# Attention and a mixture of experts on one core: tokens stored as two 16-bit planes and turned by transfers

## The chip, the core and the metric

The kernel runs on one core of a Trainium2 chip, as one launch. The metric is the device time in microseconds, the median of timed runs. The engines are TensorE (PE in the rows; its weight loads are PEld), VectorE (DVE), ScalarE (ACT), GpSimd (POOL) and SyncE (SP), which here only issues transfers.

## The reference

A local-global attention (4 batches, 8 heads, 768 positions, 64 per head) gives x of 3072 tokens by 512. A gate picks two of eight experts for each token, and the experts' outputs are added with the gate's weights:

```python
logits = x @ w_gate
noisy = logits + np.log1p(np.exp(x @ w_noise)) * noise
top2 = np.argpartition(-noisy, 2, axis=1)[:, :2]
...                                   # softmax over the two: top2_w
for e in range(8):
    for k in range(2):
        mask = top2[:, k] == e
        h = np.maximum(x[mask] @ w1[e], 0.0)          # 512 -> 1024
        out[mask] += top2_w[mask, k, None] * (h @ w2[e])
```

## The kernel before, in words

Attention runs over 24 blocks of 128 tokens, in steps of two pairs of heads; a written order (the loop over `n`, with `at`, `tick` and `finish`) puts routing steps between its matmuls. `gate_t(g)` stores block g of x to the DRAM tensor `xd` (rows of 512 float32) from SP and turns it on TensorE for the gate; `gate_l` and `gate_s` finish the gate's logits. `route(r)` turns the logits of a segment of blocks into lists of token rows per expert. Segment 2 (`CLOSE`, up to block 16) closes the first 512 tokens of expert 0, and four gathers fetch them by GpSimd's indirect transfers (`gather`, `xg`).

Each expert works on a fixed number of tokens (812 down to 768), in tiles of 128: 7 tiles for experts 0 to 4, 6 for the last three. Expert 0 is done plainly: `turn` transposes a gathered tile on TensorE, four 128x128 blocks into one PSUM bank, and ScalarE and VectorE split it into a high and a low part (`xh`, `xl`); `up(c, f)` and `down(0, t)` are its two products. Each product is three passes of matmuls on the split parts.

Experts 1 to 7 use a product of seven block products in place of eight (`first`, with `TERMS`), which wants sums of blocks of the tokens and of the weights. `tokens(e, t)` takes tiles t and t + 3 (for t = 3 tile 6 alone), transposes them on TensorE (the loops at L1229 and L1235) and makes the sums t1 to t4 on VectorE, with the parts cut by ScalarE and VectorE (`cut`, L194 and L195). `weights(e, c)` does the like with GpSimd's subtractions (L1189 to L1192). `first(e, before)` loops over four blocks c of features; in each, `between(c, slot)` runs the jobs of a table `ahead` at slots 4 to 7, between products of six matmuls. `second(e)` runs the down products, and between them spreads `prepare(e + 1)`, the list of jobs that makes the next expert's tokens. `put` scales a result and adds it to the output rows by GpSimd's indirect transfers.

Every engine takes its instructions in the order in which the program is written; waits are by semaphores between engines. SP's queue holds the loads of weights (`load_w`, four `raw` buffers), the stores of x and the clearing of the output. GpSimd's queue holds gathers, scatters, the weights' sums and, for segments 0 to 2, the routing masks (L505). The stores of a block wait for the last of its heads (`norm`, L837); the next user of the same `ys` buffer waits for the store. The last part, a loop under `tc.If(left > 0)`, serves tokens beyond an expert's capacity; it did not run.

Of the kernel before, what the change touches and what calls it, by code (L numbers as in the profile page):

```python
# [15 lines left out]
U32 = mybir.dt.uint32  # L16
AF = mybir.ActivationFunctionType
# [3 lines left out]
P = 128  # L21
# [13 lines left out]
def tile_local_global_attention_then_moe(  # L35
# [51 lines left out]
    xd = dram.tile([N + DUMP, Dm], F32, name="xd")  # L87
# [120 lines left out]
    xg = {}  # L208
# [10 lines left out]

    def gather(e, t, n=DUMP + N):  # L220
        if e >= E or t >= tiles(e):
            return
        r = rows(e, t)[0]
        xg[e, t] = gp.tile([r.shape[0], Dm], F32, name="xg", bufs=5)
        nc.gpsimd.indirect_dma_start(  # L225
            out=xg[e, t], out_offset=None, in_=xd[:n],
            in_offset=bass.IndirectOffsetOnAxis(ap=r, axis=0),
            bounds_check=n - 1, oob_is_err=False)

# [6 lines left out]
    def rank():  # L236
# [4 lines left out]
        more_ = gp.tile([P, Dm], F32, name="xg", bufs=5)[:, :n * n].rearrange("p (r e) -> p r e", r=n)  # L241
# [11 lines left out]
        for x in range(2):  # L253
            b = gp.tile([P, Dm], F32, name="xg", bufs=5)[:, :n * n * TT].rearrange("p (r t e) -> p r t e", r=n, t=TT)
# [6 lines left out]
    def rest():  # L261

        x = gp.tile([P, Dm], F32, name="xg", bufs=5)
# [18 lines left out]
    def turn(e, t, ps=None):  # L282
        if t >= tiles(e):
            return
        x = xg.pop((e, t))
# [16 lines left out]
    XR, XT, LS = {}, {}, {}  # L302
# [30 lines left out]
    def gate_l(g):  # L333
        j = partner(g)
# [56 lines left out]
    def route(r):  # L391
# [135 lines left out]
        def marks(i):  # L527
            b = gp.tile([P, Dm], F32, name="xg", bufs=5)
# [36 lines left out]
        if r == CLOSE:  # L565
# [14 lines left out]
    with ExitStack() as actx:  # L580
# [126 lines left out]
        def empty_rows():  # L707
            nc.gpsimd.memset(zero, 0.0)
            o = xd[:DUMP].rearrange("(p r) d -> p r d", p=P)
            nc.sync.dma_start(o, zero[:, None, :].to_broadcast(o.shape))  # L710
# [297 lines left out]
    with ExitStack() as mctx:  # L1008
# [51 lines left out]
        def put(e, t, ps):  # L1060
# [4 lines left out]
            ins = nc.gpsimd.indirect_dma_start(  # L1065
                out=out, out_offset=bass.IndirectOffsetOnAxis(ap=r, axis=0),
                in_=y, in_offset=None, bounds_check=N + DUMP - 1, oob_is_err=True, compute_op=OP.add)
            for o in added[e]:
                tc.declare_no_dep(ins.ins, o.ins, reason="an expert's tokens are all different")
            added[e].append(ins)  # L1070
# [4 lines left out]
        def down(e, t):  # L1075
# [6 lines left out]
            for f in features if e else range(FC):  # L1082
# [3 lines left out]
                if n == 3 * FC:  # L1086
                    put(e, t, ps)
# [123 lines left out]
        def tokens(e, t, banks):  # L1211
# [11 lines left out]
            def one():  # L1223
                if t < 3:
                    x1, x2 = (bank_at(banks.pop(0)).rearrange("p (k t) -> p k t", k=KC) for _ in range(2))
                    for ps, j in ((x1, t), (x2, t + 3)):
                        x = xg.pop((e, j))
                        for k in range(KC):
                            nc.tensor.transpose(ps[:, k], x[:, k * P:(k + 1) * P], ident)  # L1229
                else:  # L1230
                    x = xg.pop((e, 6))
                    r = x.shape[0]
                    ps = bank_at(banks.pop(0))[:, :KC * r].rearrange("p (k t) -> p k t", k=KC)
                    for k in range(KC):
                        nc.tensor.transpose(ps[:, k], x[:, k * P:(k + 1) * P], ident[:r, :r])  # L1235
                    x1, x2 = ps[:, :, :r // 2], ps[:, :, r // 2:]
# [4 lines left out]
                if t < 2:  # L1241
                    gather(e, fetch[5 + t])
# [4 lines left out]
            def two():  # L1247
# [3 lines left out]
                nc.vector.tensor_sub(t3, t2, t3)  # L1251
# [6 lines left out]

        def prepare(e):
            if e == 1:  # L1260
                banks = [3, 1, 0, 4, 1]
                return pair[1:] + [y for t in (1, 2, 3) for y in tokens(1, t, banks)]
            banks = [1, 2, 3, 7, 0, 4, 1]
            w = [x for c in range(2) for x in weights(e, c)]
            x = [tokens(e, t, banks) for t in range(3 + (tiles(e) > 6))]
            x = [[lambda a=a, b=b: (a(), b()), c, d] for a, b, c, d in x]
            todo = [w[0], *x[0], w[1], *x[1], *x[2]]
            if tiles(e) > 6:
                todo += x[3]
            return todo + [w[2]]  # L1270

        for t in range(3):
            for i, _ in enumerate(down(0, t)):
                if (t, i) == (2, 1):
                    for j in range(TB):
                        turn(0, TA + j, bank("sc") if j == TB - 1 else None)
                    for j in fetch[:5]:
                        gather(1, j)
        w0, w1_ = weights(1, 0), weights(1, 1)
        pair = tokens(1, 0, [2, 7])  # L1280
        ready = {0: w0[0], 1: w1_[0], 3: w0[1], 4: w1_[1], 5: w0[2], 6: w1_[2]}
        for f in range(FC):
            if f == FC - 1:
                pair[0]()
            up(1, f)
            if f in ready:
                ready[f]()
# [36 lines left out]
        def first(e, before):  # L1324
# [21 lines left out]
            def get(j):  # L1346
                return lambda: gather(e + 1, fetch[j])

            ahead = {
                (0, 4): [w[1][0]], (0, 5): [w[1][1], get(0)], (0, 6): [w[1][2], w2_(0)], (0, 7): [w2_(4)],  # L1350
# [175 lines left out]
```

## Time and profile before

| | |
|---|---|
| timed runs | 730.53, 729.93, 729.34 us; median 729.93 |
| the profiled execution, first to last instruction | 730.6 us, 16343 instructions |
| TensorE busy / its weight loads | 708.1 us (97%) / 636.3 us (87%) |
| VectorE, ScalarE, GpSimd busy | 452.6, 397.7, 275.7 us |
| granted TensorE clock | 0.994 mean |
| sizes of transfers | first load of k 464 KB, of q 256 KB; a block of x 256 KB |

The times of stages are read from the busy times of windows: attention until 140 us, the first expert's up and down products until some 220, then a pattern of a preparation (some 23 us) and four blocks of features (some 48 us) per expert, and a tail from 675 us. In rows of the chain the first number is the start, the second the time on the chain; in rows of instructions the first is the start, the second the duration, and the bracket at the end the idle time before it with what ended it. In rows of groups a mean in ns stands before the second bar.

### The profile page before, as it was taken

What the parts mean: (1) busy time and instruction counts of PE and PEld (TensorE: products, weight loads), DVE (VectorE), ACT (ScalarE), POOL (GpSimd) and SP (SyncE); (2) the same over time, 40 slices, a digit from 0 to 9 for tenths busy, and PEclk for the clock granted to TensorE, in tenths of its full rate; (3) what the DMA queues carried; (4) which work ended last, traced back from release to release, by engine and by line L of the source; (5) the groups of instructions that cost most, each with busy time, mean ns of one, the idle gap of its engine ahead of it and who ended that gap; (6) DMA issues with size and microseconds to landing.
All of it is one profiled execution on the core that took longest, in us unless ns stands there. A gap on an engine that the chain in (4) does not pass through costs nothing.

```text
span 730.6 us, 16343 instructions
## 1 busy us (share of the span) xinstructions
PE 708.1 (97%) x5953; PEld 636.3 (87%) x5953; DVE 452.6 (62%) x1473; ACT 397.7 (54%) x901; POOL 275.7 (38%) x292
## 2 busy tenths in 40 slices
PE   7999999999999999999999999999999999999993
PEld 5878888777899999999989998999898899889983
DVE  7668788858947487457636762766367557637500
ACT  6888787652335564456445644655455446445510
POOL 2230404410182463255436524551645345442221
PEclk9999999999999999999999999999999999999997
DMA  9996779962082463246443634471446436533243
GB/s 268 315 307 194 231 221 310 285 227 106 23 242 78 55 177 96 55 96 146 117 67 103 147 95 75 130 172 32 88 144 148 85 86 146 128 59 88 29 49 42
DMA packets 84393, 99.75 MB, mean 137 GB/s; under 512 B 6100, under 2 KB 51284, under 8 KB 84304
## 3 DMA queue, kind: packets, MB, share of 16 engines
q1 hardware_dynamic: 72896, 72.53, 32.0%
q0 software_dynamic: 11264, 25.83, 19.8%
q8 instruction: 49, 0.80, 0.5%
q10 hardware_dynamic: 144, 0.26, 0.2%
q14 instruction: 40, 0.33, 0.1%
HBM read 71.01 MB, written 27.59 MB: 135 GB/s over the span
## 4 chain that ended last, share of the span: by engine, by line
PE 65%; issue 6%; POOL 3%; DVE 3%; ACT 2%; DMA 1%; POOLq 0%; ACTq 0%; DVEq 0%
PE av L1084 23%; PE bank L1337 22%; PE av L1107 9%; PE bank L1229 3%; PE at L1054 2%; PE sc L1054 2%; POOL out_dram L1065 2%; PE av L821 1%; DVE wall L195 1%; PE bank L1130 1%; DMA out_dram<-zero,ids 1%; DVE w2l L195 1%; ACT hh L1035 1%; POOL wall L505 1%; PE at L800 1%
## 5 line engine op out<-in xcount | busy, mean ns | idle before, releaser
L1337 PE MATMUL bank<-xh,wall 128*128 128x384 f32 (+4 forms) x784 | 215.6, 342 | 0.8 <-DVE aside L1370 0.6
L1337 PEld LDWEIGHTS bank<-xh,wall 128*128 128x128 f32 x784 | 143.4, 188 | 5.6 <-DVE wall L195 1.4
L1337 PE MATMUL bank<-xl,wall 128*128 128x384 f32 (+4 forms) x392 | 133.4, 340 | 0.0
L1065 POOL DMA_INDIRECT out_dram<-y,ids x40 | 62.8, 1570 | 154.2 <-ACT y L1064 123.1
L1084 PE MATMUL av<-w2h,hh 128*128 128x512 f32 x304 | 120.5, 396 | 0.0
L1084 PE MATMUL av<-w2h,hl 128*128 128x512 f32 x304 | 119.1, 392 | 0.0
L1084 PE MATMUL av<-w2l,hh 128*128 128x512 f32 x304 | 119.1, 392 | 0.0
L195 DVE TENSOR_TENSOR wall<-raw,wall 128x512 fp32r<-128x512 f32 (+1 forms) x84 | 73.4, 880 | 50.3 <-ACT wall L194 50.2
L1039 DVE SCALAR_TENSOR_TENSOR hl<-bank,hh 128x384 fp32r<-128x384 f32 (+4 forms) x84 | 47.1, 560 | 61.4 <-ACT hh L1035 61.3
L194 ACT ACTIVATE wall<-raw 128x512 fp32r<-128x512 f32 (+1 forms) x84 | 58.1, 700 | 46.4 <-POOL raw L1192 46.4
L225 POOL DMA_INDIRECT xg<-xd,ids x53 | 57.6, 1087 | 63.4 <-DVE place L245 47.4
L787 ACT ACTIVATE a<-ns,mx 128x168 f32<-128x168 f32 (+1 forms) x192 | 67.9, 422 | 17.4 <-DVE mx L784 16.5
L1337 PEld LDWEIGHTS bank<-xl,wall 128*128 128x128 f32 x392 | 73.9, 188 | 2.7
L1035 ACT ACTIVATE hh<-bank 128x384 fp32r<-128x384 f32 (+4 forms) x84 | 41.6, 496 | 57.9 <-DVE bank L1405 39.5
L1084 PEld LDWEIGHTS av<-w2h,hl 128*128 128x128 f32 x304 | 57.1, 188 | 12.6
L1084 PEld LDWEIGHTS av<-w2l,hh 128*128 128x128 f32 x304 | 57.2, 188 | 9.2 <-DVE w2l L195 0.3
L1084 PEld LDWEIGHTS av<-w2h,hh 128*128 128x128 f32 x304 | 57.1, 188 | 9.1
L784 DVE CUSTOM_DVE_ANT_0 ns<-sc,bias 128x168 f32<-128x168 f32 (+1 forms) x188 | 51.7, 320 | 17.0 <-PE sc L770 8.6
L821 PE MATMUL av<-vs,at 128*64 128x65 f32 (+1 forms) x768 | 58.0, 225 | 0.8 <-issue 0.8
L821 PEld LDWEIGHTS av<-vs,at 128*64 128x64 f32 (+1 forms) x768 | 51.1, 136 | 3.3 <-issue 2.9
L1191 POOL TENSOR_TENSOR raw<-raw 128x256 f32<-128x256 f32 x28 | 22.4, 799 | 82.0 <-DVE wall L195 81.7
L821 PE MATMUL av<-vp,at 40*64 40x65 f32 (+1 forms) x640 | 50.4, 223 | 0.7 <-issue 0.6
(213 smaller groups left out, 1417.2 us busy)
## 6 DMA issues: line engine op xcount, KB each, us to landing
raw<-in_w SPq DMA_DIRECT2D x64, 256.0 KB
raw<-in_w SPq DMA_DIRECT2D x32, 512.0 KB
out_dram<-zero SPq DMA_DIRECT2D x14, 512.0 KB
vs<-in_v SPq DMA_DIRECT2D x24, 260.0 KB
xd<-y SPq DMA_DIRECT2D x24, 256.0 KB
qbuf<-in_q SPq DMA_DIRECT2D x23, 256.0 KB
ks<-in_k SPq DMA_DIRECT2D x20, 272.0 KB
vp<-in_v SPq DMA_DIRECT2D x20, 195.0 KB
```

The costliest lines, as they stand in the source:

```text
L194: nc.scalar.activation(hi, src, AF.Copy)
L195: eng.tensor_sub(lo, src, hi.bitcast(F32))
L225: nc.gpsimd.indirect_dma_start(out=xg[e, t], out_offset=None, in_=xd[:n], in_offset=bass.IndirectOffsetOnAxis(ap=r, axis=0), bounds_check= ...
L784: nc.vector.tensor_tensor_reduce(out=ns[x][:, s, :w], in0=ps[:, s], in1=bias[:, u + x, s] if i else bias0[:, u + x, s], scale=-scale, scal ...
L787: nc.scalar.activation(A[n + x][:, s * w:(s + 1) * w], ns[x][:, s, :w], AF.Exp, bias=mx[x][:, s:s + 1], scale=-1.0)
L821: nc.tensor.matmul(ps[s * Q:(s + 1) * Q, h], a[r:z, part * P + q0:part * P + q0 + Q], t[r:z, c], start=k == 0 and (n == 1 or h == 0), stop ...
L1035: nc.scalar.activation(inner(e)[0][j][:, f, :src.shape[1]], src, AF.Relu)
L1039: nc.vector.scalar_tensor_tensor(lo, src, 0.0, hi.bitcast(F32), op0=OP.max, op1=OP.subtract)
L1065: ins = nc.gpsimd.indirect_dma_start(out=out, out_offset=bass.IndirectOffsetOnAxis(ap=r, axis=0), in_=y, in_offset=None, bounds_check=N + ...
L1084: nc.tensor.matmul(ps, x[j][:, f, cols], w[:, f], start=n == 0, stop=n == 3 * FC - 1)
L1107: nc.tensor.matmul(to, w[:, f, cols], x[:, f], start=n == 0, stop=n == 3 * FC - 1)
L1337: nc.tensor.matmul(ps, wb[c % 2][u][:, 2 * a + k], x[v][:, 2 * b + k], start=start and n == 0, stop=stop and n == 5, skip_group_check=True)
```

## The change

- `xd` holds, per row, the 512 low 16-bit halves of the words and then the 512 high halves. GpSimd makes these planes from a block of x in four copies of 128 x 256 (`halved`), and SP stores the result at `gate_l`, one call later than before.
- Expert 0's gathered tiles are joined back to words by GpSimd (`whole_words`, four copies a tile) and turned on TensorE as before. For the first four tiles the joining follows the four gathers in `route(CLOSE)`; for the other three it stands at step (0, 2) of `down(0, t)`.
- Experts 1 to 7: each gathered tile is turned by one transposing transfer from SP (`flip`), and ScalarE writes the two planes, interleaved to words, into the tile's old buffer (`weave`). `tokens` reads that from SBUF; TensorE's transposes and one ScalarE copy per pair go.
- Gathers, flips and weaves get places of their own in the tables (`moves`: `get`, `tip`, `mix`). All gathers of an expert are now in the tables of the expert before. Expert 0's three first scatters are held back until the up products of its last tokens. `rank` comes before expert 0's last gathers.
- `xg` has 7 buffers for 5, the new `xt` has 4, and the area for the descriptors of GpSimd's transfers is set to 4096 bytes a partition.

```diff
-    xd = dram.tile([N + DUMP, Dm], F32, name="xd")
+    xd = dram.tile([N + DUMP, 2 * Dm], U16, name="xd")
...
+    def words(x):
+        return x.bitcast(U16).rearrange("p (d h) -> p h d", h=2)
+    def planes(x):
+        return x.rearrange("p (h d) -> p h d", h=2)
+    def halved(to, frm):
+        for c in range(KC):
+            c = slice(c * P, (c + 1) * P)
+            nc.gpsimd.tensor_copy(to[:, :, c], frm[:, :, c])
...
+    def whole_words(e, t):
+        if t >= tiles(e):
+            return
+        m = full(e, t)
+        x = xg.pop((e, t))[:m]
+        if t < TA:
+            xw[e, t] = gp.tile([P, Dm], F32, name="xg", bufs=7)[:m]
+        else:
+            xw[e, t] = gp.tile([P, 2 * Dm], U16, name="xt", bufs=4).bitcast(F32)[:m]
+        halved(words(xw[e, t]), planes(x.bitcast(U16)))
+    def flip(e, t):
+        if (e, t) not in xg:
+            return
+        m = full(e, t)
+        y = gp.tile([P, 2 * Dm], U16, name="xt", bufs=4)
+        xt[e, t] = y[:, :2 * KC * m].rearrange("p (c t) -> p c t", t=m)
+        nc.sync.dma_start_transpose(xt[e, t], xg[e, t].bitcast(U16)[:m])
+    def weave(e, t):
+        if (e, t) not in xt:
+            return
+        m = full(e, t)
+        x = xg.pop((e, t))[:, :KC * m]
+        nc.scalar.activation(words(x), xt.pop((e, t)).rearrange("p (h k) t -> p h (k t)", h=2), AF.Copy)
+        xw[e, t] = x.rearrange("p (k t) -> p k t", k=KC)[:, :, :min(P, CAPS[e] - t * P)]
...
     def gate_t(g):
         x = XR.pop(g).rearrange("p h d -> p (h d)")
-        nc.sync.dma_start(xd[DUMP + g * P:DUMP + (g + 1) * P], x)
+        stored[g] = gp.tile([P, 2 * Dm], U16, name="xt", bufs=4)
+        halved(planes(stored[g]), words(x))
...
     def gate_l(g):
+        nc.sync.dma_start(xd[DUMP + g * P:DUMP + (g + 1) * P], stored.pop(g))
...
             for t in range(TA):
                 gather(0, t, DUMP + z * P)
                 yield LAST
+            for t in range(TA):
+                whole_words(0, t)
+                yield
...
+        rank()
         for t in range(TB):
             gather(0, TA + t)
-        rank()
...
-                    x1, x2 = (bank_at(banks.pop(0)).rearrange("p (k t) -> p k t", k=KC) for _ in range(2))
-                    for ps, j in ((x1, t), (x2, t + 3)):
-                        x = xg.pop((e, j))
-                        for k in range(KC):
-                            nc.tensor.transpose(ps[:, k], x[:, k * P:(k + 1) * P], ident)
+                    x1, x2 = xw.pop((e, t)), xw.pop((e, t + 3))
...
-                nc.scalar.activation(t3, x1[:, :2], AF.Copy)
-                nc.vector.tensor_sub(t1, x2[:, :2], t3)
+                nc.vector.tensor_sub(t1, x2[:, :2], x1[:, :2])
...
+        early = {(0, 0): [get[0]], (0, 1): [get[1]], (0, 2): [lambda j=j: whole_words(0, TA + j) for j in range(TB)],
+                 (1, 0): [get[2]], (1, 1): [get[3]], (2, 0): [tip[0]], (2, 1): [tip[1]], (2, 3): [tip[2]],
+                 (2, 2): [lambda j=j: turn(0, TA + j, bank("sc") if j == TB - 1 else None) for j in range(TB)]}
...
+        ready = {0: [w0[0], get[4], get[5]], 1: [w1_[0], tip[3], get[6]], 2: [mix[0], tip[4]], 3: [w0[1], mix[1]],
+                 4: [w1_[1], tip[5], *held[:1]], 5: [w0[2], mix[2], *held[1:2]], 6: [w1_[2], tip[6], mix[3]],
+                 7: [pair[0], *held[2:]]}
...
             ahead = {
+                (0, 4): [w[1][0]], (0, 5): [w[1][1], get[0]], (0, 6): [w[1][2], w2_(0)], (0, 7): [w2_(4)],
+                (1, 4): [w[2][0], tip[0]], (1, 5): [w[2][1], get[1]], (1, 6): [w[2][2], get[2]],
+                (1, 7): [w2_(1), mix[0]],
+                (2, 4): [w2_(5), w[3][0], tip[1]], (2, 5): [w[3][1], get[3], tip[2]], (2, 6): [w[3][2]],
+                (2, 7): [w2_(2), mix[1], tip[3]],
+                (3, 4): [w2_(6), get[4]], (3, 5): [w2_(3), mix[2]], (3, 6): [w2_(7), get[5], tip[4]],
+                (3, 7): [mix[3], get[6]],
             }
...
-    nc = bacc.Bacc("TRN2", target_bir_lowering=False, num_devices=1)
+    nc = bacc.Bacc("TRN2", target_bir_lowering=False, num_devices=1, dynamic_dma_scratch_size=4096)
```

## Rows read from the trace of the kernel before

**Rows 1.** Busy time by window: window, its length, each engine, clock, DMA share, GB/s
```profile
0.00:140.00 140.00, 132.77 (x2543) 113.64 (x2544) 108.89 (x712) 110.11 (x308) 36.64 (x71) 1.00 0.87 265
190.00:220.00 30.00, 30.00 (x172) 26.59 (x173) 18.53 (x51) 10.91 (x21) 19.69 (x19) 1.00 0.58 161
223.00:241.00 18.00, 18.00 (x129) 17.33 (x128) 13.46 (x31) 8.69 (x20) 1.02 (x2) 1.00 0.25 79
354.00:377.00 23.00, 23.00 (x159) 21.51 (x157) 14.07 (x31) 11.83 (x29) 5.28 (x4) 1.00 0.21 49
447.00:495.00 48.00, 48.00 (x253) 44.32 (x252) 28.08 (x46) 25.84 (x53) 27.23 (x26) 1.00 0.59 133
```

**Rows 2.** Waits of TensorE: waiting line, releaser, us in total, times, longest
```profile
PE sc L770 <- DMA ks<-in_k: 5.0, 1, 5.0
...
PE bank L1337 <- DVE aside L1370: 0.6, 1, 0.6
```

**Rows 3.** The chain that ended last, 278 to 300 us: start, us, what
```profile
280.64 1.13 PE bank L1337 x6
281.77 1.40 PE av L1084 x6
283.18 0.87 PE bank L1229 x8
...
297.67 0.36 PE bank L1235 x4
```

**Rows 4.** Groups of instructions by form, one of ScalarE and one of VectorE
```profile
L194 ACT ACTIVATE xh<-aside 128x1024 fp32r<-128x1024 f32 x21 | 22.3, 1062 | 4.7 <-DVE aside L1251 4.7
...
L837 DVE TENSOR_TENSOR y<-av,den 128x256 f32<-128x256 f32 x48 | 20.0, 417 | 6.9 <-DMA xd<-y 6.2
```

**Rows 5.** Instructions of ScalarE, 468 to 473 us
```profile
469.71 0.48 ACT L1376 ACTIVATE aside<-bank 128x390 f32<-128x390 f32 x1
471.42 0.50 ACT L1035 ACTIVATE hh<-bank 128x390 fp32r<-128x390 f32 x1 [1.23 <-DVE bank L1405]
```

**Rows 6.** DMA queues: packets, MB, time of their packets as share of 16 engines
```profile
q1 hardware_dynamic: 72896, 72.53, 32.0%
q0 software_dynamic: 11264, 25.83, 19.8%
```

**Rows 7.** SP's queue at the start: the first load of k
```profile
0.80 0.45 SPq L596 DMA_DIRECT2D ks<-in_k  x1
```

**Rows 8.** Groups of GpSimd's instructions by form
```profile
L505 POOL TENSOR_SCALAR wall<-iota_p,aside 128x128 fp32r<-128x128 f32 x34 | 21.8, 656 | 64.2 <-DVE aside L513 64.2
L1192 POOL TENSOR_TENSOR raw<-raw 128x256 f32<-128x256 f32 x28 | 21.4, 763 | 0.0
...
L642 POOL TENSOR_SCALAR_AFFINE_SELECT dist<-dist 64x240 f32<-64x240 f32 x1 | 0.4, 386 | 0.0
```

**Rows 9.** VectorE, 151 to 154 us: the last part of block 21 of x
```profile
152.28 0.42 DVE L837 TENSOR_TENSOR y<-av,den 128x256 f32<-128x256 f32 x1
```

**Rows 10.** TensorE, 162 to 164 us: turns of expert 0's tiles 2 and 3, first up
```profile
162.01 1.25 PE L290 MATMUL sc<-ident,xg 128*128 128x128 f32 x8 [0.40 <-DVE wall L293]
...
163.95 0.50 PE L1054 MATMUL at<-wall,xh 128*128 128x512 f32 x1 [0.54 <-ACT wall L292]
```

**Rows 11.** GpSimd, 196 to 200 us: the gathers of expert 0's tiles 4 and 5
```profile
196.68 1.00 POOL L225 DMA_INDIRECT xg<-xd,ids  x1 [47.37 <-DVE place L245]
197.98 1.23 POOL L225 DMA_INDIRECT xg<-xd,ids  x1 [0.30 <-issue]
```

**Rows 12.** The chain that ended last, 205 to 210 us
```profile
205.93 2.95 PE av L1084 x12
208.88 1.65 PE at L1054 x12
```

**Rows 13.** VectorE's subtractions of weights, 454 to 462 us
```profile
454.74 0.69 DVE L195 TENSOR_TENSOR wall<-raw,wall 128x512 fp32r<-128x512 f32 x1
...
460.15 1.22 DVE L195 TENSOR_TENSOR w2l<-raw,w2h 128x512 fp32r<-128x512 f32 x1
```

More of the change, by code (lines that the diff above doesn't have):

```diff
@@ L1058, in up, with put @@
             evict(0, f, c, ps)
-        def put(e, t, ps):
+        def put(e, t, ps, held=None):
             r, g = rows(e, t)
@@ L1064, in put, with scatter, down @@
             nc.scalar.activation(y, ps, AF.Copy, scale=g)
[L1065 to L1070, printed above, removed]
+            def scatter():
+                ins = nc.gpsimd.indirect_dma_start(
+                    out=out, out_offset=bass.IndirectOffsetOnAxis(ap=r, axis=0),
+                    in_=y, in_offset=None, bounds_check=N + DUMP - 1, oob_is_err=True, compute_op=OP.add)
+                for o in added[e]:
+                    tc.declare_no_dep(ins.ins, o.ins, reason="an expert's tokens are all different")
+                added[e].append(ins)
+            if held is None:
+                scatter()
+            else:
+                held.append(scatter)
         added = [[] for _ in range(E)]
         features = [f for c in range(NU) for f in (c, c + NU)]
-        def down(e, t):
+        def down(e, t, held=None):
             ps = bank("av")
@@ L1086, in down @@
                 if n == 3 * FC:
-                    put(e, t, ps)
+                    put(e, t, ps, held)
                 if n % 6 == 0:
@@ L1257, in tokens, with moves @@
             return [one, same, two, three]
+        def moves(e):
+            return [[lambda j=j, f=f: f(e, fetch[j]) for j in range(len(fetch))] for f in (gather, flip, weave)]
         def prepare(e):
+            get, tip, mix = moves(e)
             if e == 1:
-                banks = [3, 1, 0, 4, 1]
-                return pair[1:] + [y for t in (1, 2, 3) for y in tokens(1, t, banks)]
-            banks = [1, 2, 3, 7, 0, 4, 1]
+                x, y, z = (tokens(1, t) for t in range(1, 4))
+                get, tip, _ = moves(2)
+                return [*pair[1:3], mix[4], get[0], pair[3], *x[:2], mix[5], get[1], x[2], mix[6], get[2], x[3],
+                        *y[:2], get[3], y[2], get[4], y[3], *z[:3], get[5], tip[0], z[3], get[6], tip[1]]
             w = [x for c in range(2) for x in weights(e, c)]
-            x = [tokens(e, t, banks) for t in range(3 + (tiles(e) > 6))]
+            x = [tokens(e, t) for t in range(3 + (tiles(e) > 6))]
             x = [[lambda a=a, b=b: (a(), b()), c, d] for a, b, c, d in x]
             todo = [w[0], *x[0], w[1], *x[1], *x[2]]
+            if e > 2:
+                todo = [w[0], tip[5], *x[0][:2], mix[4], x[0][2], w[1], tip[6], *x[1][:2], mix[5], x[1][2]]
+                todo += [*x[2][:2], mix[6], x[2][2]]
             if tiles(e) > 6:
@@ L1270, in prepare @@
             return todo + [w[2]]
-        for t in range(3):
[L1273 to L1278, printed above, removed]
+        get, tip, mix = moves(1)
+        held = []
+        early = {(0, 0): [get[0]], (0, 1): [get[1]], (0, 2): [lambda j=j: whole_words(0, TA + j) for j in range(TB)],
+                 (1, 0): [get[2]], (1, 1): [get[3]], (2, 0): [tip[0]], (2, 1): [tip[1]], (2, 3): [tip[2]],
+                 (2, 2): [lambda j=j: turn(0, TA + j, bank("sc") if j == TB - 1 else None) for j in range(TB)]}
+        for t in range(3):
+            for i, _ in enumerate(down(0, t, held)):
+                for x in early.get((t, i), []):
+                    x()
         w0, w1_ = weights(1, 0), weights(1, 1)
-        pair = tokens(1, 0, [2, 7])
-        ready = {0: w0[0], 1: w1_[0], 3: w0[1], 4: w1_[1], 5: w0[2], 6: w1_[2]}
+        pair = tokens(1, 0)
+        ready = {0: [w0[0], get[4], get[5]], 1: [w1_[0], tip[3], get[6]], 2: [mix[0], tip[4]], 3: [w0[1], mix[1]],
+                 4: [w1_[1], tip[5], *held[:1]], 5: [w0[2], mix[2], *held[1:2]], 6: [w1_[2], tip[6], mix[3]],
+                 7: [pair[0], *held[2:]]}
         for f in range(FC):
-            if f == FC - 1:
-                pair[0]()
             up(1, f)
-            if f in ready:
-                ready[f]()
+            for x in ready[f]:
+                x()
         def second(e):
```

61 lines of the change are left out of this document (29 added, 32 removed).

## The prediction

> **What bounds the kernel now.** I read the busy times by stage first [rows 1]. TensorE is busy 48.00 of 48.00 us in the stage from 447 to 495 us, and the other windows of the experts look the same; the attention stage has 132.77 of 140. In the 48 us stage VectorE has 28.08 us of work, ScalarE 25.84, GpSimd 27.23 and the DMA engines a share of 0.59. Then the waits of TensorE [rows 2]: the longest in the expert stages is 0.6 us in total, so nothing but TensorE's own queue sets the pace there. Then the chain of waits over one preparation of an expert [rows 3]: it stays on TensorE, and the transposes of the gathered tokens stand in it as pieces of their own. So time taken out of TensorE's queue in the expert stages comes off the end, unless something else gets late.
>
> **Part 1: the transposes that go.** Experts 1 to 4 have 7 token tiles and 5 to 7 have 6: 42 full tiles and 4 small ones. A tile pair is one piece of 8 transposes, 0.87 us in the chain [rows 3]. That is also what TensorE's queue loses, because the chain stays on it. 21 pieces of 0.87 are 18.3 us and 4 small ones of 0.36 (297.67) are 1.4: **19.7 us off TensorE**. Expert 0's 28 tile transposes stay.
>
> **Part 2: ScalarE, VectorE and the flips in the expert stages.** Each of the 46 flipped tiles needs one ScalarE pass over 1024 elements (weave). The nearest row is a 128x1024 pass at 1062 ns [rows 4]; 42 x 1.06 and four small ones of at most 0.35 make 46 us, and a shorter copy per tile pair goes. Per 48 us stage that is about 4 us more on 25.84. The pass put at the end of a block of features falls just before 469.71, and by 471.42 ScalarE waits 1.23 us for VectorE anyway [rows 5], so I cost it at nothing; without that cover it costs 1.06 us a time. VectorE's subtractions now read SBUF and not PSUM; no row shows the pair side by side, and I take nothing either way, since VectorE isn't the last one there. With 3 us fewer on TensorE in each preparation, VectorE's 14.07 us of 23 become 14 of 20, still under. Two places have no slack. In front of expert 1 VectorE has 13.46 of 18 us, which become 13.5 of 15. In expert 1's own first block two weaves (2.1 us) come in, while one gather of 1.0 us goes. I take 1 us for both together; bounds are 0 and 4.1 (3.0 not gained and 1.1 net).
>
> The flip itself, a transposing transfer from SP, is in no row. Its destination has 128 x 8 = 1024 runs of 256 bytes. The queue table [rows 6] gives 32.0% of 16 x 730.6 us for 72896 packets, 51 ns each, and 205 ns for the software queue's 11264. With 1024 packets on 16 engines the data take 3.3 us at 51 ns, 13 us at 205; with only 128 packets 0.4 us. Latency: the two first loads, of 464 and 256 KB, one of them issued by SP at 0.80 [rows 7], had both landed when TensorE's wait of 5.0 us ended [rows 2]; of these 4.2 us, 2.3 are data (720 packets of 51 ns on 16 engines). So from issue to landing a flip takes 1.9 + 0.4 = 2.3 us to 1.9 + 13 = 14.9; I take 1.9 + 3.3 = 5.2, by the row of its own queue. How late may it be? Where flip and weave stand closest (slots 4 and 7 of one block), TensorE passes three products of 1.1 us, then four more and two groups of 6 down matmuls (1.40) before it needs the ScalarE copy behind the weave [rows 3]: 3.3 + 7.2 = 10.5 us. Off go 1.3 us until the weight cut ahead of it is done, and 1.06 + 0.48 for weave and copy: 7.7 us. At 5.2 no stall. While SP waits for a gather, the weight loads behind it wait too; they are issued four buffers ahead, so nothing. DMA share: 46 x 3.3 = 152 us, 21% of the span on top; in the 48 us stage 0.59 becomes at most 0.9.
>
> The Trainium skill speaks more lightly of the flip: Advanced Engine Details and Errata, section DMA Advanced Topics, says that transposing transfers on trn2 run about as fast as plain ones (350 to 400 GB/s). By that, an estimate from that page, 256 KB take 0.7 us of data instead of 3.3, and the sum is the same, since the flip is hidden at either. No run here shows one yet.
>
> **Part 3: GpSimd's copies on the path.** GpSimd now makes 24 x 4 copies to store x and 7 x 4 to join expert 0's tiles, each 128 x 256 16-bit elements. Call one c. From below, a one-input select of 240 elements took 386 ns; from above, a two-input operation of 256 took 763, and the compare 656 for 128, which would be 1.31 us for 256 [rows 8]. I take **c = 0.50**: nearest to the one-input row, with something for VectorE beside it.
>
> Place A, the end of attention. Before, the four gathers were issued well ahead of the turns. Now GpSimd's order behind the gathers for tiles 0 to 2 is: halving of block 21, which waits for VectorE until 152.28 + 0.42 [rows 9]; the gather of tile 3 (1.3 with its gap); joining of tile 0; halving of block 22; joining of tiles 1 to 3. That ends at 152.7 + 1.3 + 24c. From the last tile's transposes to the first up matmul it took 1.5 us (162.45, half way through the block of 8, to 163.95) [rows 10]. So the experts start at 155.5 + 24c instead of 163.95: **3.55 us late** at 0.50, 0.8 at 0.386, 9.8 at 0.76, 23 at 1.31. Nothing else is queued on TensorE there.
>
> Place B, expert 0's tiles 4 to 6. Gathers start at 196.68 and run every 1.3 us [rows 11]; the scatters are held back, and two of expert 1's gathers go first, so joining starts at 203.2 and ends at 203.2 + 12c. TensorE waits in order; then come 0.37 us of transposes and 6 down matmuls, half of the 2.95 us that stand there now, before up(1, 0), which started at 208.88 [rows 12]. 205.0 + 12c against 208.88: **2.1 us late** at 0.50, 0.75 at 0.386, 5.2 at 0.76, 11.8 at 1.31. The last turn's ScalarE and VectorE steps fit in those 6 matmuls within 0.5 us. The held scatters and later gathers only fill GpSimd's 10 idle us of 30.
>
> During attention the halving adds 96c = 48 us to GpSimd's 36.64 of 140 [rows 1]. The store now waits for it, one step later; the y buffer was already late before (VectorE waited 6.2 us for the store) [rows 4], so I expect that to even out. Side by side the two engines slow each other: VectorE's 128x512 subtraction took 0.69 us alone and 1.22 while GpSimd worked [rows 13]. VectorE has 31 us spare in 140, so I take 1 us; bounds 0 and 6.
> The Trainium skill's GPSIMD Engine Reference, section 8, names this: GpSimd shares its SBUF interfaces with VectorE, and it advises VectorE for elementwise work. The trace agrees (0.69 against 1.22 us). By its section 3.1 (512 elements in 0.77 us) a copy would be 0.38 us, an estimate from that page, and the sum would be 4.3 us lower.
>
> The smaller descriptor area and the moved x-load of the overflow path cost nothing visible: at most five gathers in a row are in flight, and the overflow branch does not run. [...]
>
> **Sum.** -19.7 + 3.55 + 2.1 + 1 + 1 = -12.05. The profiled execution spans 730.6 us, 0.7 above the median of 729.93 (730.53 is the slowest timed run). 730.6 - 12.05 - 0.7 = **718 us**.
>
> **Rivals.**
> *Full gain.* c = 0.386 and no other loss: 19.7 - 1.55 = 18.2, 711.7 us. For it: the one-input row. Against: VectorE works beside the copies.
> *Gain eaten by copies.* c = 0.76, the two-input row: 15.0 + 2 lost, 727 us. For it: every larger GpSimd row is that slow.
> *Slow copies, slower.* c = 1.31: 34.8 + 2 lost, 747 us. For it: the compare row with its 5 ns an element; against: it has a scalar operand and rounds. It decides from 36c - 12.3 + 2 = 19.7, c = 0.84.
> *Late flips, slower.* The transfer needs more than 7.7 us, ScalarE stands at the weave with TensorE's evictions behind it. For each us above, four weaves in each of five preparations lose one: 20 us. At 8.7 the kernel needs 738 us; at 8.3 nothing is gained. For it: 205 ns a packet; against: SP's own 51 ns, and depth of seven gather buffers.
> *No change of bound.* The DMA engines fill up, weight loads come late, and the gain goes back as waits on raw: around 730.
>
> **Chances.** Forecast (713 to 723) 0.48; full gain 0.13; eaten 0.15; late flips 0.12; slow copies 0.08; DMA 0.04. A measurement can tell 0.2%, so 728.5 to 731.4 is no change. Faster 0.48 + 0.13 + 0.13 = 0.74; same 0.06; slower 0.20. The range 710.5 to 735 leaves out most of the two slower rivals.
>
> **What would show it.** Right: no transposes of xg on TensorE after 210 us; TensorE without gaps in the 48 us stages, the stages between shorter by 3.0 us; the first up matmul at 167.5 and up(1, 0) some 5.7 us late against before; copies of about 0.5 us. Wrong: idle TensorE in the blocks of features behind ScalarE evictions (late flips), copies above 0.8 us, or GpSimd masks late at 135 us.

## The result and the profile after

The changed kernel takes 718.89 us (median of 716.03 to 720.23), the kernel before 729.85 beside it: a ratio of 0.9841 [0.982, 0.9863], 11.0 us faster. The forecast was 718. The total is right, but several of its terms are wrong, in opposite directions, as the traces show. The ratios here are of fast executions alone: one of 17 of the kernel before, on another chip, took 2300.86 us, and one of twelve of e4 741.42 us, and neither is in a ratio.

The page of the changed kernel: busy time and instructions by engine, then packets and queues (packets, MB, share of 16 engines).

```profile
PE 692.7 (97%) x5769; PEld 618.3 (86%) x5769; DVE 457.1 (64%) x1473; ACT 440.0 (61%) x922; POOL 323.3 (45%) x416
...
DMA packets 129913, 111.10 MB, mean 155 GB/s; under 512 B 51578, under 2 KB 96762, under 8 KB 129824
...
q1 hardware_dynamic: 118416, 83.84, 42.9%
q0 software_dynamic: 11264, 25.89, 20.1%
```

TensorE has 15.4 us less to do, ScalarE 42 us and GpSimd 48 us more. SP's queue went from 72896 packets to 118416 [rows 6]: 45,520 packets for 46 flips, some 1,000 a flip. The time of that queue's packets went from 32.0% of 730.6 us to 42.9% of 716.9, 74 us more, or 1.6 us a flip.

The new operations, from the groups by form of the changed kernel (count, busy us, mean ns, idle time before them and what ended it):

```profile
L275 ACT ACTIVATE xg<-xt 128x1024 uint16<-128x1024 uint16 x42 | 57.8, 1380 | 17.2 <-DMA xt<-xg 17.0
...
L235 POOL COPY xt<-y 128x256 uint16<-128x256 uint16 x96 | 35.2, 405 | 49.0 <-DVE y L890 46.9 <-DVE we L508 2.0
L235 POOL COPY xg<-xg 128x256 uint16<-128x256 uint16 x16 | 6.4, 482 | 0.0
```

A weave is a third longer than the 128x1024 pass it was sized by [rows 4], and in front of the weaves ScalarE stands idle for 17 us, waiting for flips. The copies are shorter than the 0.50 us forecast; in a row they overlap, so that twelve take 4.7 us, 0.39 each.

Waits of TensorE in the changed kernel, where before one of 0.6 us was the longest in the expert stages [rows 2], and ScalarE's waits for flips:

```profile
PE av L1144 <- ACT aside L1176: 2.3, 1, 2.3
PE av L1144 <- ACT hh L1088: 1.7, 1, 1.7
PE av L1167 <- ACT aside L1176: 1.5, 1, 1.5
PE bank L1397 <- ACT aside L1438: 0.9, 1, 0.9
...
PE sc L338 <- POOL xg L235: 0.6, 1, 0.6
...
ACT xg L275 <- DMA xt<-xg: 19.6, 13, 4.2
```

The first four are waits for evictions by ScalarE that stood behind a weave or a cut. This is the sign that the prediction named for late flips; the first of them is left when the flips are in time (e2, e6).

**Where they stand.** The table has the length of each stage, from the start of its first matmul to that of the next one's, read from TensorE's rows of three executions (the third is e6, the fastest of the experiments; the last row ends at the last scatter's piece of the chain). "Without" is the stage of before less its transposes, 0.87 us a piece and 0.36 a small one.

| stage | before | without | changed | three moves |
|---|---|---|---|---|
| start to first up | 163.95 | 163.95 | 163.21 | 163.62 |
| first up to up(1, 0) | 44.77 | 44.77 | 45.45 | 45.48 |
| up(1, 0) to expert 1's blocks | 32.48 | 29.51 | 34.77 | 33.09 |
| expert 1 | 64.90 | 61.93 | 61.00 | 60.96 |
| expert 2 | 70.88 | 67.91 | 71.72 | 67.69 |
| expert 3 | 69.61 | 66.64 | 67.03 | 66.41 |
| expert 4 | 68.58 | 65.97 | 65.90 | 65.94 |
| expert 5 | 65.91 | 63.30 | 63.43 | 63.24 |
| expert 6 | 65.20 | 62.59 | 63.97 | 62.46 |
| expert 7 to last scatter | 74.41 | 74.41 | 74.41 | 74.43 |

Of 19.7 us, 5.3 are lost in front of expert 1, 3.8 in expert 2 and 1.4 in expert 6. At the two places where GpSimd's copies are on the path next to nothing is lost in sum: 0.74 us are gained up to the first up matmul and 0.68 lost from there to up(1, 0). At the last scatter the changed kernel is 9.8 us ahead. Another 3.9 us of the difference between the two spans lie behind that scatter, in GpSimd's closing DRAIN row: 8.39 us before (L1521), 4.43 in the changed kernel (L1585) and at most 4.60 in the ten experiments. The timed medians, 11.0 us apart, don't have them in full: every span on record lies some 1.7 us under its execution's time, so the median execution of the kernel before spans some 728.1 us, and the profiled one, 730.6, is 2.5 us longer. Whether the smaller descriptor area has a part in the shorter DRAIN was not tried.

The two places of the copies, from the changed kernel's timeline (start, duration, and in brackets the idle time before and what ended it):

```profile
153.87 1.67 POOL L235 COPY xg<-xg 128x256 uint16<-128x256 uint16 x4
...
157.33 4.74 POOL L235 COPY xg<-xg 128x256 uint16<-128x256 uint16 x12
...
161.30 1.22 PE L338 MATMUL sc<-ident,xg 128*128 128x128 f32 x8 [0.56 <-POOL xg L235]
...
163.21 0.50 PE L1107 MATMUL at<-wall,xh 128*128 128x512 f32 x1 [0.54 <-ACT wall L340]
...
195.91 1.02 POOL L243 DMA_INDIRECT xg<-xd,ids  x1 [32.49 <-DVE place L293]
...
202.22 4.71 POOL L235 COPY xt<-xg 128x256 uint16<-128x256 uint16 x12
```

The first up matmul comes 0.74 us earlier than before [rows 10], and the gathers of expert 0's last tiles 0.77 us earlier [rows 11]. That is one pair of executions: in the eight other traces in which these copies are made once, the first up matmul comes between 163.46 and 164.87 us.

The two larger losses, in the changed kernel's chain (start, us, what):

```profile
225.85 7.78 DMA xt<-xg
...
233.74 0.07 ACT xg L275
...
234.24 0.39 ACT aside L1176
...
240.54 3.04 PE av L1144 x12
...
336.17 8.07 DMA xg<-xd,ids
344.26 6.97 DMA xt<-xg
...
353.06 1.71 PE av L1144 x5
...
355.42 14.54 PE av L1167 x96
```

Before expert 1 the flip of the last tile, 48 rows and so 96 KB, went out at 225.85. It stood on SP behind three weight loads, two of which had waited 2.6 and 1.0 us for VectorE to free a buffer, and it then took 7.78 us. In expert 2 a gather took 8.07 us, the flip behind it 6.97, and TensorE stood still until 353.06. What follows is slow too. The windows of the changed kernel (columns as in [rows 1]; the number after the engines is the granted clock):

```profile
352.00:355.00 3.00, 1.92 (x6) 1.00 (x7) 1.96 (x4) 2.35 (x5) 0.61 (x1) 1.00 0.96 326
355.00:360.00 5.00, 5.00 (x26) 4.90 (x26) 2.73 (x7) 2.87 (x4) 2.83 (x3) 0.66 0.90 151
```

At a granted clock of 0.66, a mean over stretches at 1.2 and at 2.4 GHz, 5.0 us do the work of 3.3. So of the 3.8 us of expert 2 1.7 are slow clock, and the other 2.1 are waiting, 1.7 of them in front of 353.06.

### The profile page after: what moved, and what is told of

It is laid out like the page before. It is cut to its first block, busy times and chain, and to the rows that moved or that the text cites. A ratio compares the mean times of both kernels' runs of the same rounds, so it can differ in the third digit from the quotient of the medians.

```text
span 716.9 us, 16231 instructions
## 1 busy us (share of the span) xinstructions
PE 692.7 (97%) x5769; PEld 618.3 (86%) x5769; DVE 457.1 (64%) x1473; ACT 440.0 (61%) x922; POOL 323.3 (45%) x416
## 3 DMA queue, kind: packets, MB, share of 16 engines
q1 hardware_dynamic: 118416, 83.84, 42.9%
## 4 chain that ended last, share of the span: by engine, by line
PE 64%; DVE 10%; issue 8%; DMA 7%; POOL 5%; ACT 5%; POOLq 0%; SPq 0%; ACTq 0%; DVEq 0%
PE bank L1397 20%; PE av L1144 19%; PE av L1167 7%; PE av L874 4%; PE sc L823 4%; PE at L853 3%; DMA xt<-xg 3%; DMA xg<-xd,ids 2%; DVE wall L196 2%; PE at L1107 1%; ACT hh L1088 1%; DVE w2l L196 1%; POOL out_dram L1120 1%; DVE ns L837 1%; DMA xd<-xt 1%
## 5 line engine op out<-in xcount | busy, mean ns | idle before, releaser
L275 ACT ACTIVATE xg<-xt 128x1024 uint16<-128x1024 uint16 (+3 forms) x46 | 60.0, 1307 | 19.7 <-DMA xt<-xg 19.6
L235 POOL COPY xt<-y 128x256 uint16<-128x256 uint16 x96 | 35.2, 405 | 49.0 <-DVE y L890 46.9
```

What stands on the lines that cost most here:

```text
L275: nc.scalar.activation(words(x), xt.pop((e, t)).rearrange("p (h k) t -> p h (k t)", h=2), AF.Copy)
```

## The experiments

The first theory: TensorE loses its time behind flips that go out late, because they stand in a chain of queues (gather on GpSimd behind sums of weights, flip on SP behind that gather and behind loads). The rivals: ScalarE's 60 us of weaves are the loss, wherever they stand; or the DMA engines are too full, so that a flip is slow wherever it is put. The runs were made on three chips, on which the kernel before took 733.95, 730.24 and 733.89 us, so ratios are compared; 0.1% is 0.73 us.

| run | median, us | ratio to before |
|---|---|---|
| changed kernel | 718.89 | 0.9841 [0.982, 0.9863] |
| e0, again | 720.28 | 0.9856 [0.9832, 0.988] |
| e1, early gathers | 722.87 | 0.985 [0.983, 0.9871] |
| e2, last tile first | 717.53 | 0.9782 [0.9762, 0.9801] |
| e3, both and flips | 716.2 | 0.9761 [0.9741, 0.978] |
| e4, joining twice | 737.41 | 1.0037 [1.0011, 1.0064] |
| e5, weaves twice | 744.87 | 1.021 [1.0195, 1.0225] |
| e6, three moves | 711.1 | 0.9742 [0.9728, 0.9757] |
| e7, sums early | 711.99 | 0.9746 [0.9733, 0.9758] |
| e8, planes twice | 724.81 | 0.9876 [0.9839, 0.9912] |
| e9, sums ahead of cut | 713.47 | 0.9725 [0.9708, 0.9743] |

**e0: the same kernel again.**

> The changed kernel once more, unchanged, as the measure for the other runs of this chip. A ratio of 0.982 to 0.986 to the kernel before. Both theories: the same. If flips that come late or in time by chance make the spread of its times (716.0 to 720.2 us so far, against 729.3 to 730.5 of the kernel before), the stretches in which TensorE waits behind a weave are others in this execution than in the first.

Its six times go from 716.26 to 722.5, those of before beside it from 729.13 to 731.42. The losses sit elsewhere: expert 3 has 69.29 us (67.03 in the first execution), expert 6 66.49 (63.97), and expert 2 only 68.47 (71.72). So which flip is too late changes from one execution to the next, and several are close to it.

**e1: all gathers early.**

```diff
-(0, 5): [w[1][1], get[0]], (0, 6): [w[1][2], w2_(0)], (0, 7): [w2_(4)],
-(1, 4): [w[2][0], tip[0]], (1, 5): [w[2][1], get[1]], ...
+(0, 5): [w[1][1], get[0]], (0, 6): [w[1][2], w2_(0), get[1]], (0, 7): [w2_(4), get[2]],
+(1, 4): [get[3], w[2][0], tip[0]], (1, 5): [w[2][1], get[4]], ...
```

> The changed kernel (718.9 us) with one thing moved: in the table of the blocks of features of experts 2 to 6, the seven gathers for the next expert are issued between (0, 5) and (2, 4) and no longer between (0, 5) and (3, 7). Late chain (mine): in expert 2's fourth block the gather went out at 336.17 and took 8.1 us, the flip behind it 7.0 us, and TensorE then waited 1.7 + 0.3 + 0.5 + 1.5 us; with the gather in place before, these go, some 3.8 us, and 0 to 1 us in the other experts: 714 to 716. ScalarE's load (rival): the 60 us of weaves are what is lost, wherever they stand; nothing moves, 718 to 720. DMA load (rival): flips are slow because 16 engines are full, and gathers in front of other traffic only push that back: 718 to 722.

No gain, 0.985. Expert 2 is indeed 3.1 us shorter (68.63), but expert 3 is 2.9 longer (69.88; 69.29 in e0) and expert 5 2.2 longer (65.65). In this kernel's timeline four of seven gathers go out in a row, and the first flip is among them:

```profile
386.32 1.10 POOL L243 DMA_INDIRECT xg<-xd,ids  x1 [0.16 <-issue]
...
390.82 1.42 SPq L267 DMA_TRANSPOSE xt<-xg  x1
...
402.11 1.34 ACT L275 ACTIVATE xg<-xt 128x1024 uint16<-128x1024 uint16 x1 [3.91 <-DMA xt<-xg]
...
403.84 0.45 PE L1397 MATMUL bank<-xh,wall 128*128 128x396 f32 x1 [1.76 <-ACT aside L1438]
```

From 390.82 to its landing at 402.02, that flip needed 11.2 us, more than any in the changed kernel's chain, and the eviction behind its weave kept TensorE waiting for 1.76 us. It isn't the only one. e1's chain:

```profile
322.19 10.16 DMA xt<-xg
...
390.82 11.20 DMA xt<-xg
...
526.30 10.77 DMA xt<-xg
```

Here the rival with the DMA load is right: how long a flip takes depends on what runs beside it. These are first flips of a table. Counted by its packets in the trace (1024 of 256 bytes), the first flip of the five tables for experts 2 to 6 ends 6.2 to 10.1 us after its issue in e1, and 4.7 to 4.9 us in the changed kernel.

**e2: expert 1's last tile first.**

```diff
-0: [w0[0], get[4], get[5]], 1: [w1_[0], tip[3], get[6]], ...
-4: [w1_[1], tip[5], ...], 5: [w0[2], mix[2], ...], 6: [w1_[2], tip[6], mix[3]],
+0: [w0[0], get[4], get[5], get[6]], 1: [w1_[0], tip[3]], ...
+4: [mix[2], w1_[1], tip[5], tip[6], ...], 5: [w0[2], ...], 6: [w1_[2], mix[3]],
```

> The changed kernel with the last tile of expert 1 earlier: its gather stands ahead of the weights' subtractions of block 1 on GpSimd, the weave of the third tile one step earlier, and the flip of the last tile behind that, ahead of two weight loads on SP. Late chain (mine): before expert 1 TensorE waited 0.5, 1.5 and 2.3 us behind the weave of that tile, whose flip took 7.8 us after SP came to it at 225.9; issued some 3 us earlier, 3 to 4.5 us come back: 714.5 to 716. ScalarE's load: the same passes in the same stretch, nothing comes back, 718 to 720. If instead the sums of the weights become late (1.3 us later on GpSimd), an eviction waits behind them and up to 1 us is lost: 720.

0.9782, 4.3 to 5.4 us below the unchanged kernel by the ratios and so a little more than the 3 to 4.4 that the theory expected, but not all of it from the place that was moved: up(1, 0) to expert 1 takes 33.06 us, 1.7 less than 34.77, and a wait of 2.24 us remains there although the flip is in time. In the profiled execution, the fastest of the five, expert 2 has no wait above 0.25 us and takes 68.75 us, 3.0 less than 71.72.

**e3: both, and the flips ahead of the loads.** The same two edits, and at (2, 4), (2, 5) and (2, 7) `tip` stands first; `tip[4]` moves to (3, 4).

> Both moves of the two runs before, and in experts 2 to 6 the flips of the second to fifth tile stand ahead of the weight loads of their slot on SP and no longer behind them. Late chain (mine): all waits of TensorE behind flips go, some 5 us before expert 1, 3.8 in expert 2, 1.4 in expert 6: 709 to 711. ScalarE's load: 718 to 720. DMA load: the flips collide with more weight loads, some of which come late: 715 to 722, with waits of TensorE behind the cuts of weights.

0.9761: 6 to 7 us better than the changed kernel by the ratios, not the 8 to 10 expected. TensorE still waits 2.8 us behind L1438, in the same slots as in e1: the flips are not behind the loads any more, but beside a crowd of gathers.

**e6: three moves only.** e2's edit, and in the table for experts 2 to 6:

```diff
-(2, 4): [w2_(5), w[3][0], tip[1]], (2, 5): [w[3][1], get[3], tip[2]],
+(2, 4): [get[3], tip[1], w2_(5), w[3][0]], (2, 5): [w[3][1], tip[2]],
```

> The changed kernel with the last tile of expert 1 earlier (as in the second run), and in experts 2 to 6 only two more moves, both at (2, 4): the fourth gather ahead of the subtractions of weights on GpSimd, and the second flip ahead of the weight load on SP. The other gathers stay where they are, so that they don't come in a row of seven. Order of queues (mine): the waits of expert 2's fourth block (3.8 us in the first execution) and expert 6's third (0.9 us) are gone for good, and none comes in their place: 3 to 5 us below the unchanged kernel, and a spread of its times below 3 us. DMA load (rival): a flip takes 7 to 11 us beside gathers wherever it stands; at most 1 us better than the second run with the last tile alone.

711.1 us, 9.2 below the unchanged kernel on the same chip (720.28; 8.3 by the ratios), and the times go from 710.2 to 712.56. That is about twice the 3 to 5 expected. The expectation had counted the waits of the changed kernel's first execution alone, and e0's, beside this one, has others: 7.1 us above "without" in experts 2 to 6, and 2.4 more than e6 in front of expert 1. So most of the loss was the order of the queues. Its waits of TensorE and of ScalarE:

```profile
PE av L1144 <- ACT aside L1176: 2.3, 1, 2.3
PE m L393 <- ACT pair L380: 0.7, 1, 0.7
...
ACT xg L275 <- DMA xt<-xg: 1.3, 2, 0.8
```

ScalarE's waits for flips fall from 19.6 to 1.3 us with the same 46 weaves and the same flips. In the table all six experts' stages are as short as "without", or shorter: with the flips in time, the whole of the 19.7 us is there, except in front of expert 1. Of the rivals, ScalarE's load falls. The DMA load remains as what makes a flip long beside gathers (e1, e3) or behind loads (the 7.78 us above). In the timeline of this kernel the second and the fourth flip of expert 2's table go out at 327.77 and 338.88, 24.6 and 35.7 us after its blocks begin, where the changed kernel had 334.88 and 344.26, 30.5 and 39.8 us after:

```profile
327.77 1.24 SPq L267 DMA_TRANSPOSE xt<-xg  x1
...
338.88 1.24 SPq L267 DMA_TRANSPOSE xt<-xg  x1
```

On the whole it is the start that moved and not the duration, as the trace's packets show. In experts 3 to 6 too the second flip goes out 4.8 us or more and the fourth 1.1 to 3.0 us earlier behind the start of the blocks than in the changed kernel. From its issue to its last packet the fourth flip of experts 2 to 6 takes 2.3 to 6.1 us in the changed kernel and 3.2 to 5.0 in e6; only in expert 2 is it much shorter as well (3.4 against 6.1). Which of the two moves at (2, 4) did how much was not separated.

**e5: each weave twice.**

```diff
+        for _ in range(2):
             nc.scalar.activation(words(x), y, AF.Copy)
```

> The changed kernel with each of the 46 weaves made twice by ScalarE (60 us of work more, same result). ScalarE's load (rival): weaves stand in front of evictions that TensorE waits for, so most of 46 x 1.31 comes through: 20 to 60 us, 739 to 779. Late chain (mine): in the blocks of features ScalarE has room, and a second pass costs only where the first was already late: two or three places of 1.3 us, and before expert 1, where ScalarE and VectorE set the pace, four passes of 1.3: 724 to 730. Hidden throughout, as the prediction had the first pass: 719.

0.0354 above e0, 26 us: my range was far too low, and the rival's was met. The waits of TensorE:

```profile
PE bank L1399 <- ACT aside L1440: 12.0, 8, 2.3
...
PE av L1169 <- ACT hh L1090: 3.1, 2, 1.9
PE bank L1399 <- DVE aside L1434: 2.7, 4, 1.0
```

46 passes of 1.31 us cost 26, 0.56 each. So the first weave just fits (e6 shows that it costs nothing when its flip has landed), and a second one doesn't. The changed kernel's 31.58 us of ScalarE's work in the 48 us from 447 to 495 say nothing of that; it is the place in front of an eviction that is full.

**e4: the joining twice.** `halved(words(...), planes(...))` in `whole_words` stands twice.

> The changed kernel with GpSimd's joining of expert 0's seven tiles made twice (28 copies more, same result). Copies on the path (mine): at both places TensorE already stands for the last joined tile, so each added copy counts in full; at the 0.39 us that a copy took in a row, 16 make 6.3 us at the end of attention and 12 make 4.7 us before the last tokens of expert 0: 729 to 730. As the prediction had a copy (0.50 us): 14 us, 733. Hidden (rival): the copies cost nothing because other work covers them; then at most 4 us: 719 to 723.

1.0037, against 0.9841 and 0.9856 unchanged: 13 to 14 us for 28 copies, 11 expected. The first up matmul comes at 170.75, in the three other kernels of that chip at 164.60 to 164.87: 6.0 us for 16 copies, as expected. Between there and up(1, 0) 8.1 us are added, where 12 copies explain 4.7. The copies in this kernel's timeline:

```profile
211.94 9.33 POOL L235 COPY xt<-xg 128x256 uint16<-128x256 uint16 x24
```

The windows behind TensorE's waits at the two places:

```profile
172.00:180.00 8.00, 8.00 (x50) 5.90 (x50) 4.26 (x29) 1.68 (x4) 0.00 (x0) 0.79 0.95 350
...
220.00:224.00 4.00, 3.67 (x10) 2.65 (x11) 0.34 (x1) 0.32 (x1) 3.54 (x7) 0.50 0.68 158
224.00:228.00 4.00, 4.00 (x22) 3.90 (x21) 0.36 (x1) 1.50 (x3) 1.24 (x2) 0.68 0.73 179
```

The 24 copies take 9.33 us, 0.39 each; the rest is the granted clock after TensorE's waits, down to 0.50. So the copies are on the path at both places, and the changed kernel lost next to nothing there only because they are short.

**e8: the storing copies twice.** `halved(planes(stored[g]), words(x))` in `gate_t` stands twice.

> The changed kernel with the four copies that store a block of x made twice (96 copies, 35 us of GpSimd, more; same result). Covered (mine): GpSimd has the room in attention and VectorE has 31 us to spare, so all but the copies of blocks 21 and 22, which stand in GpSimd's queue among and behind the last gathers, cost nothing: up to 8 x 0.37 = 3.0 us, 0 to 3 us in all, with the first up matmul up to 3 us later. Shared access (the prediction's term): VectorE is slowed beside the copies, the last scores and masks come later too, and 1 to 6 us are lost on top: 4 to 9 us.

0.9876, 1.5 to 2.6 us above the unchanged kernel by the ratios; the interval holds both of that kernel's ratios, so no loss is clear in the total. Three of its six executions, 720.47 to 722.89 us, have a mean granted clock of 0.995, the other three, 726.73 to 729.48, one of 0.988 or 0.989. The profiled one, 726.73, has this window behind TensorE's wait at the first up matmul (the clock there is 1.00 in the changed kernel):

```profile
164.00:172.00 8.00, 7.58 (x39) 5.50 (x40) 4.87 (x29) 2.49 (x6) 5.77 (x16) 0.57 0.35 132
```

The first up matmul comes at 168.26, 3.9 us later than in e9 on the same chip (164.39) and 4.8 to 5.1 later than in the two executions of the changed kernel, not up to 3: sixteen added copies and not eight stand in GpSimd's queue between the masks and the last joining, and some of them only fill time in which it waits for VectorE (2.2 us in e9). The masks begin at 137.81, 1.15 us later than in e9, and 0.2 to 1.4 later than in the ten traces with these copies made once. So what VectorE loses by then beside the added copies is at most 1.4 us.

**e7 and e9: what holds TensorE in front of expert 1.** Both on top of e6: the four subtractions of the first pair of tiles are taken out of `tokens` and issued in the up products, in e7 at `ready` 5 and 7, in e9 at 4, ahead of `w1_[1]`.

```diff
-4: [mix[2], w1_[1], tip[5], tip[6], ...], ... 7: [pair[0], ...]
+4: [mix[2], pair[0], soon[0], w1_[1], tip[5], tip[6], ...], ... 7: [...]
```

> As the run before, and the four subtractions of expert 1's first pair of tiles are made on VectorE during the up products of expert 0 instead of behind them. VectorE's chain (mine): in front of expert 1 it goes subtraction, cut, three subtractions, cut, wait for ScalarE's 1024, cut: 4.6 us a pair, 3 pairs, which with the last cut ends after TensorE's products; TensorE waits 2.2 us at its end in every run so far. With 1.6 us of it moved out of the chain the wait falls to 0.6 and the kernel gains 1.6 us. Weave or flip (rival): the last tile's data set that end; then nothing changes.

> As the kernel with three moves (711.1 us), and the four subtractions of expert 1's first pair of tiles stand on VectorE ahead of the cut of weights that waits 3.8 us for GpSimd's sums, not behind it as in the run before this one, where the chain began only 0.4 us earlier. VectorE's chain (mine): the chain of three pairs of 4.6 us, behind whose last cut by ScalarE an eviction stands, starts 1.3 to 1.6 us earlier, TensorE's last wait of 2.2 us falls to 0.6 to 0.9, and the kernel gains 1.3 to 1.6 us: 709.5 to 710. The other way (rival): the wait is set by something that starts with the last up product, and stays 2.2 us: 711.

e7 gains nothing (711.99 against 711.1 on the same chip): its subtractions landed behind a cut of weights on VectorE that waits 3.78 us for ScalarE. In e9 they are done by 223.5, and yet the wait is 1.87 us, 0.4 less than 2.25, where 0.6 to 0.9 was expected. So my theory of a chain on VectorE alone fell. The total decides less: the ratio's interval overlaps e6's, and in the profiled executions of e7 and e9 TensorE's clock fell behind that wait (last section). e9's timeline:

```profile
227.78 1.03 DVE L196 TENSOR_TENSOR xl<-xg,xh 128x512 fp32r<-128x512 f32 x2
230.56 1.23 DVE L196 TENSOR_TENSOR xl<-aside,xh 128x1024 fp32r<-128x1024 f32 x1 [1.75 <-ACT xh L195]
...
227.94 1.37 ACT L275 ACTIVATE xg<-xt 128x1024 uint16<-128x1024 uint16 x1
229.18 0.39 ACT L1176 ACTIVATE aside<-av 128x300 f32<-128x300 f32 x1
229.47 1.05 ACT L195 ACTIVATE xh<-aside 128x1024 fp32r<-128x1024 f32 x1
```

VectorE is free at 228.8 and waits for a cut that ScalarE makes only after a weave and an eviction. Freed of one engine's work, the chain waits on the other. From the second pair on, a pair takes 4.6 us in all these kernels (VectorE's 1024-element cut at 230.56, 235.17 and 239.77), with both engines in it. What a shorter order of the two would do was not tried.

## Why the prediction was right, and where it was wrong

The gain is there for the reason forecast, and its size came out by luck: terms that were too dear by 7.6 us in sum stand against terms that were too cheap by 9.9.

- **What bounds the kernel, and part 1: right.** TensorE's queue sets the pace, and a piece is worth 0.87 us. The six experts' stages of e6 are 0.03 to 0.23 us below "without", expert 1's by 1.0, where TensorE had waited 0.6 us before [rows 2].
- **Part 3, the copies: too dear.** The step that failed is c = 0.50. The rows give 0.39, the one-input row of 386 ns [rows 8] almost exactly, with nothing to add for VectorE. At place A the forecast was 3.55 us late, and the matmul came 0.74 early; by the prediction's own formula 0.39 gives 164.9, 0.9 late. It counted 24 copies behind 154.0, but block 21's four had been made before the last gather; with 20 the formula gives 163.3, and 163.21 was measured. Place B is at 208.83 in the chain, where A and B together were forecast 5.65 us late, against 208.88 [rows 12].
- **VectorE beside GpSimd, 1 us:** not to be seen at the first up matmul. A sign that the prediction named did come: the masks begin at 136.96 us, 1.6 later than before (135.37). But VectorE's largest group in attention takes 319 ns a piece against 320, the 1.6 us are made good by the first up matmul, and e8 allows at most 1.4 us for 35 us of added copies. What delays the masks stays open.
- **In front of expert 1, 1 us with an upper bound of 4.1: 5.3.** The step that failed compared VectorE's busy time with the length of the stage. The stage is a chain of handovers between ScalarE and VectorE, 4.6 us a pair, so its 3.0 us less on TensorE were never to be had in full (read from the rows of e6 and e9; no run shortened that chain); the late flip of the last tile came on top, and e2 and e6 took 1.7 us of the 5.3 back.
- **The weave: 60 us and not 46,** hidden as forecast, but without a margin (e5).
- **The flip: its start was not asked for, and its duration was not one number.** Forecast were 5.2 us from issue to landing, 3.3 of them data, with a stall from 7.7. The queue's rows give 1.6 us of data a flip. The chains show 5.26 and 6.97 us from issue to landing for full tiles and 7.78 for the small last one, and 10.2 to 11.2 beside the gathers of e1, so 5.2 was in the middle of a wide spread. What failed is the sentence on SP waiting for a gather: it counted what the gather holds up behind the flip and not that the flip itself is held up, by a gather that takes 3.3 to 8.3 us (median 5.0) and that stands behind GpSimd's sums, and by loads that wait for their buffers. 5.6 us were lost by it in experts 2 to 6. The Trainium skill's Advanced Engine Details and Errata, section DMA Advanced Topics, says that transposing transfers on trn2 are as fast as plain ones. In one chain gather and flip of the same 256 KB took 8.07 and 6.97 us, so the trace agrees as far as these two go. Undisturbed, the data were quicker than the sum had them: the flip issued at 546.98 has its 1024 packets within 1.1 us, not 3.3.
- **The rival of late flips** took place in part: not four weaves in each preparation, but two or three places in an execution, and not the same ones in e0 as in the first.

In the sum the copies were 5.7 us and VectorE 1 us too dear, the front of expert 1 was 4.3 and the flips 5.6 too cheap, and expert 1's own blocks gave 0.9 that nobody had counted: -12.05 - 5.7 - 1 + 4.3 + 5.6 - 0.9 = -9.75, against -9.8 in the profiled pair up to the last scatter; the medians are 11.0 apart, and the 1.2 us between are part of what lies behind that scatter or of the spread of single executions.

## What to carry to other kernels

When a step on TensorE becomes a chain of transfers and a pass on another engine, count the lateness of its start, queue by queue, before its duration: what the issuing engine has in front of it, and what that waits for. Put transfers ahead of work that waits, but spread them, since a bunch of gathers makes each transfer slower (flips of up to 11.2 us in e1). A stage in which two engines hand over to each other is as long as the chain of handovers; busy shares don't show it. A wider spread of times after a change is itself a sign that something now arrives just in time.

## What the runs showed of the hardware

A wait of TensorE can cost nearly twice its length, or just its length. In e6 it waits 2.25 us in front of expert 1 and goes on at full clock; in e7 it waits 1.89 us at the same place and gets half of it. The window of e6:

```profile
240.00:242.00 2.00, 2.00 (x11) 1.60 (x10) 1.45 (x8) 0.66 (x2) 1.61 (x2) 1.00 1.24 156
```

Two windows of e7:

```profile
240.00:242.00 2.00, 2.00 (x6) 1.56 (x5) 1.37 (x8) 0.66 (x2) 1.62 (x2) 0.50 1.16 181
242.00:244.00 2.00, 2.00 (x8) 1.64 (x8) 0.00 (x0) 0.00 (x0) 0.29 (x1) 0.79 1.18 368
```

At 0.50, which is 1.2 GHz, 6 matmuls fit where 11 did, and e7 needs 34.28 us from up(1, 0) to expert 1 against 33.09, with the shorter wait. e9 does the same behind its wait of 1.87 us and needs 34.64:

```profile
240.00:242.00 2.00, 1.90 (x6) 1.52 (x7) 1.91 (x7) 0.44 (x4) 1.56 (x2) 0.71 1.40 226
242.00:244.00 2.00, 2.00 (x7) 1.51 (x6) 0.34 (x1) 0.55 (x2) 0.93 (x1) 0.50 1.11 93
```

The Trainium skill, TensorE: Matmul & The Clock Gate, section "HAM oscillation — how this bites in real kernels", says that waits for transfers between groups of matmuls can let the clock fall, so that the next group starts slow. e7, e9 and expert 2 of the changed kernel agree (the waits there are for evictions), e6 doesn't show it. Which waits are followed by it stays open.

A GpSimd copy of 256 16-bit elements, interleaving or not, takes 0.37 to 0.42 us in a row, and a ScalarE pass that interleaves 1024 of them 1.38 us, 0.3 more than a 128x1024 pass on 32-bit words.
